# Gated linear attention feeding a GLU: x in place, half-word weights and 29 fillers on one core

## The chip, the cores and the metric

The program runs on one core of one Trainium2 chip. The metric is device time in microseconds (us): the median of three runs of the whole program, and beside it the time of the one execution that the profiler recorded.

The engines by their names in the profile: PE is TensorE's matmul side and PEld its weight loads, DVE is VectorE, ACT is ScalarE, POOL is GpSimd, SP is SyncE. Each engine works through its own queue in order; semaphores tie the queues together.

## The reference, cut to what matters

```python
# q, k, v, alpha: (4, 8, 768, 48) float32: batch, heads, time, channels
for t in range(S):
    state = alpha[:, :, t, :, None] * state + np.einsum('bhd,bhe->bhde', k[:, :, t], v[:, :, t])
    y[:, :, t] = np.einsum('bhd,bhde->bhe', q[:, :, t], state)
# x = y with heads beside each other: (3072, 384)
gate = 1.0 / (1.0 + np.exp(-(x @ w_gate)))      # w_gate, w_val: (384, 1536)
val = x @ w_val
out = (gate * val @ w_out).astype(np.float32)   # w_out: (1536, 384)
```

The three weight matrices arrive as float64.

## The kernel before, in words

**Tiles.** The 3072 tokens are cut into six groups (g) of 512. In a group, the attention comes in four units (p), each of two heads: a unit's heads sit at partitions 0 to 47 and 64 to 111 of a tile of 128. The feed-forward part goes through twelve slices (f) of 128 hidden channels, so there are 72 steps. A step multiplies x of the group (three thirds of 128 channels by 512 tokens) with the slices of w_gate and w_val (line 230), takes the sigmoid on ScalarE (line 625), the product on VectorE (627), splits it into a high and a low part (628, 629), and multiplies these with the slice of w_out into three PSUM banks, `po` (637). Each matrix product is three products of float32r parts: high by high, high by low, low by high. For that x, the weights and the gated values are all kept as a high and a low part.

**A unit** of the first eight (function `unit`, lines 434 to 514) works in chunks of 128 tokens: two scans over the decays on VectorE (381, 385), keys times G (389) and queries times F (447) on VectorE or GpSimd as the tuples `KEYS` and `QUERIES` say, transposes of the keys on TensorE (402) and a ScalarE copy of them (406), matmuls for the state increments (464) and for the scores (459), a mask on VectorE (472), four state updates for each unit on VectorE (487), a multiplication of the states by the decay on GpSimd (495), and the outputs: state part (506) and score part (510) into one PSUM bank, each matmul of float32 operands being two instructions. `finish` (410) copies the output to `yt` on ScalarE (413), moves its rows by DMA into the place in x that they have among 384 channels (420), then casts a full third of x to its high part (427) and subtracts to get the low one (429). The first four units, of group 0, come before all feed-forward work; units 4 to 7 are woven into the steps of group 0, later units (`late`, line 516, in chunks of 64) into those of the groups before theirs.

**Weights** (`weight_piece`, line 328). Each of the twelve slices is loaded in two pieces of 576 columns (slice 0 in three of 384) as pairs of 32-bit words, 25 pieces in all. Two ScalarE passes (342, 343), a sign pass on VectorE or on ScalarE (349, 346, by the tuple `SIGNS`) and a shift-and-or on VectorE (351) turn a float64 into a float32; a ScalarE cast (353) makes the high part and a VectorE subtraction (355) the low one. Raw words go through a ring of four tiles.

**Order.** Nothing is ordered by hand: each piece of work is added to a `Plan` with its engine, an estimated time, a due time, and what it reads and writes. `order` (line 80) simulates the engines and always takes the ready piece with the earliest latest start; `SHIFTS` moves single due times. GpSimd and those VectorE pieces that are marked `port` are kept apart in that simulation. The resulting sequence is what each queue gets.

**Fillers** (`warm`, line 606) are bfloat16 matmuls on the identity matrix whose results nobody reads. There are `WARM` of them, the first eight at once, the others wherever the plan has TensorE idle. They write the PSUM bank that unit 4's transposes use next.

Of the kernel before, what the change touches and what calls it, by code (L numbers as in the profile page):

```python
# [40 lines left out]

WIDTH = EH + 3 * T + 1
# [7 lines left out]
class Plan:  # L50
# [14 lines left out]
    def add(self, engine, time, key, fn, reads=(), writes=(), port=False):  # L65
# [12 lines left out]
        self.parts.append((engine, time, key, fn, deps, port or engine == "gpsimd"))  # L78

    def order(self):  # L80
# [23 lines left out]
        for _ in self.parts:  # L104
            best = None
            for e, ns in waiting.items():
# [5 lines left out]
                if e == "gpsimd" and any(self.parts[m][5] and latest[m] < latest[n] and max(free["vector"], ready_at[m]) < t + self.parts[n][1]  # L112
# [93 lines left out]
def gla_then_glu(ctx: ExitStack, tc: tile.TileContext, q, k, v, alpha, rows, vc, vh, weights_in, out):  # L206
# [9 lines left out]
    with ExitStack() as fast:  # L216
        chunked(fast, tc, rows, vc, vh, weights_in, out, const, ident, flags, weights, within)
# [16 lines left out]
def chunked(ctx, tc, rows, vc, vh, weights_in, out, const, ident, flags, weights, within):  # L234
# [45 lines left out]
    r_v = ring("v", 2, CH, 2, D, early=[borrow("w8", CH, 2, D) for _ in range(2)])  # L280
    raws = [(f"raw{i}", sb.tile([P, WF // 2, 2], U32, name=f"raw{i}")) for i in range(2)]
    for _ in range(2):
        nm, t = borrow("w11", WF // 2, 2)
        raws.append((nm, t.bitcast(U32)))
    r_raw = Ring(raws)
    r_kn = ring("kn", 1, CH, P, early=[borrow("w6", CH, P) for _ in range(2)])
    r_yt = ring("yt", 2, T, early=[borrow("x1", T)])
# [16 lines left out]
    r_bank = Ring([*r_at.tiles, *r_po.tiles, *r_gv.tiles[1:]])  # L304
    ob = [(f"raw{i // 2}", raws[i // 2][1].rearrange("p a b -> p (a b)").bitcast(F32)[:, i % 2 * T:(i % 2 + 1) * T]) for i in range(NM)]
# [15 lines left out]

    plan.add("gpsimd", 1.2, None, later, writes=["later", *(("start", u) for u in range(EARLY))])
# [5 lines left out]
    def weight_piece(f, key):  # L328
        cuts = (0, DM, 2 * DM, WF) if f == 0 else (0, WF // 2, WF)
        over = before(f"w{f}") if f >= 6 else []  # L330
        for i, (lo, hi) in enumerate(zip(cuts, cuts[1:])):
            n = hi - lo
            rn, raw = r_raw.next() if f < NF - 1 else raws[i]
            raw = raw[:, 0:n]
            upper, lower = raw[:, :, 1], raw[:, :, 0]
            halves = raw.bitcast(U16).rearrange("p m (w h) -> p m w h", h=2)
            most, sign = halves[:, :, 0, 1], halves[:, :, 1, 1]
            ru, rl = (rn, "u"), (rn, "l")
            kk = key
            plan.add("sync", (0.475, P * n * 8 / RATE), None, lambda raw=raw, lo=lo, hi=hi: nc.sync.dma_start(  # L340
                out=raw.rearrange("p a b -> p (a b)"), in_=weights_in[f, :, 2 * lo:2 * hi]), writes=[ru, rl])
# [92 lines left out]
    def unit(u, g, p, t):  # L434
# [6 lines left out]
        vn, v = r_v.next()  # L441
        plan.add("sync", (0.475, P * CH * 2 * D * 4 / RATE), after(t["load"], 0.2), lambda: nc.sync.dma_start(
# [434 lines left out]
```

## Time and profile before

| what | value |
|---|---|
| median of 3 runs | 548.3 us (547.92 to 549.14) |
| profiled execution | 548.93 us, span 546.9 us |
| TensorE matmul busy | 537.1 us, 98% |
| TensorE weight load busy | 433.7 us, 79% |
| VectorE busy | 331.5 us, 61% |
| ScalarE busy | 212.5 us, 39% |
| GpSimd busy | 79.6 us, 15% |
| granted TensorE clock, mean | 0.995 |

The span runs from the first instruction to the last; the rest of the execution lies around it. Busy time is the union of the instructions' recorded times on an engine: matmuls overlap in the record, so a busy TensorE can still be waiting on a column count of its own, and a filler counts as busy as much as a product does. Shares over the whole span mix the beginning, where attention and weights keep VectorE and ScalarE full, with the long rest.

### The profile page before, as it was taken

To read this page: it belongs to the slowest core of one execution; us is meant where nothing else is said; L and a number is where in the kernel's file an instruction comes from. 1 tells how busy PE (TensorE), PEld (TensorE's weight loads), DVE (VectorE), ACT (ScalarE), POOL (GpSimd) and SP (SyncE) were. 2 spreads that over 40 slices of the span, in tenths; PEclk is the share of its full clock that TensorE was granted. 3 is DMA by queue.
4 is the path that set the end of the run, shared out by engine and by line. 5 is a ranking of instruction groups with operands and counts; after the bars stand their busy time and mean duration, and the time that the engine had idled before them with its cause. 6 is when DMAs were issued, how large, how long until landed. Compare 5 with 4: busy or idle time off the path is not lost.

```text
span 546.9 us, 10258 instructions
## 1 busy us (share of the span) xinstructions
PE 537.1 (98%) x4150; PEld 433.7 (79%) x4150; DVE 331.5 (61%) x639; ACT 212.5 (39%) x386; POOL 79.6 (15%) x99
## 2 busy tenths in 40 slices
PE   8999999999999999999999999999999999999994
PEld 3767878888888888888888888888888888888883
DVE  7999899995745774546557648557556342222221
ACT  2779899863323233223223323232323222211121
POOL 2412102102202220203202112022021010000000
PEclk9999999999999999999999999999999999999998
DMA  8855787731320321402303403203311000100001
GB/s 306 284 173 182 224 258 209 235 93 63 102 79 25 102 67 37 160 18 84 103 0 103 159 1 103 86 17 102 121 41 50 1 14 16 59 0 0 2 1 64
DMA packets 22120, 51.19 MB, mean 94 GB/s; under 512 B 3504, under 2 KB 8624, under 8 KB 22064
## 3 DMA queue, kind: packets, MB, share of 16 engines
q1 hardware_dynamic: 22064, 50.46, 29.2%
q8 instruction: 34, 0.56, 0.4%
q14 instruction: 22, 0.18, 0.1%
HBM read 41.01 MB, written 4.72 MB: 84 GB/s over the span
## 4 chain that ended last, share of the span: by engine, by line
PE 96%; DMA 1%; SPq 1%; ACT 0%; issue 0%; ACTq 0%
PE gv L230 54%; PE po L637 28%; PE gv L597 3%; PE gv L402 2%; PE at L551 2%; PE gv L608 1%; DMA v<-in_vc_dram 1%; PE at L459 1%; PE at L557 1%; PE gv L506 1%; PE gv L510 1%; SPq L439 1%; PE po L459 0%; PE gv L464 0%; PE at L506 0%; PE po L506 0%
## 5 line engine op out<-in xcount | busy, mean ns | idle before, releaser
L230 PE MATMUL gv<-x,w 128*128 128x512 f32 x1296 | 315.1, 390 | 0.0
L230 PEld LDWEIGHTS gv<-x,w 128*128 128x128 f32 x1296 | 242.9, 188 | 51.1 <-issue 0.4
L627 DVE TENSOR_TENSOR gv<-gv,sg 128x512 f32<-128x512 f32 x72 | 50.5, 701 | 157.4 <-PE gv L230 150.8
L637 PE MATMUL po<-hh,w 128*128 128x512 f32 x432 | 114.1, 395 | 0.0
L628 ACT CAST hh<-gv 128x512 fp32r<-128x512 f32 x72 | 42.9, 595 | 140.3 <-DVE gv L627 133.6
L637 PEld LDWEIGHTS po<-hh,w 128*128 128x128 f32 x432 | 79.4, 188 | 17.1
L625 ACT ACTIVATE sg<-gv 128x512 f32<-128x512 f32 x72 | 43.3, 602 | 115.9 <-PE gv L230 115.9
L585 POOL TENSOR_TENSOR vs<-st,dec 64x384 f32<-64x384 f32 x32 | 35.0, 1095 | 271.7 <-DVE st L580 270.5
L629 DVE TENSOR_TENSOR hl<-gv,hh 128x512 fp32r<-128x512 f32 x72 | 49.7, 690 | 23.4 <-ACT hh L628 21.3
L637 PE MATMUL po<-hl,w 128*128 128x512 f32 x216 | 63.5, 392 | 0.0
L637 PEld LDWEIGHTS po<-hl,w 128*128 128x128 f32 x216 | 40.2, 188 | 8.4
L580 DVE SCALAR_TENSOR_TENSOR st<-st,dec,at 128x48 f32<-128x48 f32 x128 | 33.9, 265 | 4.4 <-PE at L557 0.2
L381 DVE TENSOR_TENSOR_SCAN G<-in,d1g 128x512 f32<-128x512 f32 x22 | 32.2, 1469 | 4.9 <-DMA in<-in_rows_dram 4.2
L567 DVE TENSOR_TENSOR A<-at,mask 64x256 f32<-64x256 f32 x64 | 26.9, 420 | 3.4 <-PE at L557 2.8
L389 POOL TENSOR_TENSOR in<-in,G 128x512 f32<-128x512 f32 x17 | 22.8, 1340 | 35.6 <-DVE G L381 34.8
L385 DVE TENSOR_TENSOR_SCAN F<-in,d1f 128x512 f32<-128x512 f32 x22 | 27.6, 1256 | 0.5
L538 DVE TENSOR_TENSOR A<-A,F 64x512 f32<-64x512 f32 x32 | 24.0, 750 | 0.6
L395 ACT ACTIVATE F<-F 128x512 f32<-128x512 f32 x23 | 14.7, 639 | 17.5 <-DVE A L538 14.8
L597 PE MATMUL gv<-A,vs 128*48 128x64 f32 (+1 forms) x512 | 17.6, 221 | 0.0
L597 PEld LDWEIGHTS gv<-A,vs 128*48 128x48 f32 (+1 forms) x512 | 15.2, 123 | 2.8 <-DVE A L567 2.0
L429 DVE TENSOR_TENSOR x<-x 128x512 fp32r<-128x512 f32 x18 | 12.8, 709 | 6.2 <-ACT x L427 6.2
L608 PE MATMUL gv<-ident 128*128 128x512 bf16 x55 | 15.0, 405 | 0.0
(142 smaller groups left out, 383.7 us busy)
## 6 DMA issues: line engine op xcount, KB each, us to landing
in<-in_rows_dram SPq DMA_DIRECT2D x16, 516.5 KB, 4.2
raw<-in_w_dram SPq DMA_DIRECT2D x12, 576.0 KB, 4.1
first_w<-in_w_dram SPq DMA_DIRECT2D x10, 576.0 KB, 4.7
out_dram<-raw SPq DMA_DIRECT2D x18, 256.0 KB, 2.3
v<-in_vc_dram SPq DMA_DIRECT2D x22, 192.0 KB, 4.8
A<-in_rows_dram SPq DMA_DIRECT2D x32, 128.0 KB, 3.7
x<-yt SPq DMA_DIRECT2D x35, 96.0 KB, 2.6
in<-in_rows_dram SPq DMA_DIRECT2D x4, 772.5 KB, 4.8
```

Source lines behind the costliest of these rows:

```text
L230: nc.tensor.matmul(out=dst, lhsT=lhs(a, i), rhs=rhs(b, i), start=(n == 0 and i == 0), stop=(n == len(todo) - 1 and i == NK - 1))
L381: plan.add("vector", scan(n), t["G"], lambda: nc.vector.tensor_tensor_scan(out=G[:, ::-1], data0=az[:, n:0:-1], data1=d1g[size], initial=0 ...
L385: plan.add("vector", scan(n), after(t["G"], 0.01), lambda: nc.vector.tensor_tensor_scan(out=F, data0=az[:, 0:n], data1=d1f, initial=0.0, o ...
L567: plan.add("vector", 0.43, t["mask"], lambda pa=pa, j=j, i=i: nc.vector.tensor_tensor(out=A[other[j], j].rearrange("p (c i t) -> p i c t", ...
L580: nc.vector.scalar_tensor_tensor(out=st[:, c + 1, :], in0=st[:, c, :], scalar=dec[:, c:c + 1], in1=pas[c % 2][1][:, T // 2 + c // 2 * D:T ...
L585: plan.add("gpsimd", pool_(EH * D), t["sd"], lambda j=j: nc.gpsimd.tensor_tensor(out=vs[own[j], j], in0=st[own[j], 0:EH], in1=dec[own[j]]. ...
L597: nc.tensor.matmul(out=py[R * j:R * j + D, cs], lhsT=vs[r, j, c, :], rhs=A[r, j, cs], start=True, stop=True)
L625: plan.add("scalar", act(T), first(0.3), lambda: nc.scalar.activation(out=sg, in_=got["g"][1][:, 0:T], func=AF.Sigmoid), [got["g"][0]], [sgn])
L627: plan.add("vector", vec(T), first(0.4), lambda: nc.vector.tensor_tensor(out=pv, in0=pv, in1=sg, op=ALU.mult), [sgn], [pvn])
L628: plan.add("scalar", act(T), first(0.45), lambda: nc.scalar.copy(out=hh, in_=pv), [pvn], [hhn])
L629: plan.add("vector", vec(T), first(0.5), lambda: nc.vector.tensor_tensor(out=hl, in0=pv, in1=hh, op=ALU.subtract), [pvn, hhn], [hln])
L637: nc.tensor.matmul(out=pso_now[m][1][:, 0:T], lhsT=weights.part("o", b, f)[:, m * P:(m + 1) * P], rhs=h[a][:, 0:T], start=(f == 0 and i == ...
```

## The change

**x of the first four units in place.** The v of these units is loaded with a gap of 16 zero columns between the heads (`vg`, rows of 112), and the decayed states of the two heads are written into a tile of 96 columns per chunk, zero elsewhere, by two GpSimd multiplications in place of one. The new `in_place` issues the output in three blocks of 32 channels per unit, each into the partitions and the `po` bank where x wants them: 4 x 3 matmuls from the states with 112 rows, then 4 x 2 per head from the scores. The `yt` copy and the DMAs of these units go; high and low part of x are made straight from PSUM. Steps 0 and 1 issue their products one third of x at a time, where they took two thirds and then one. The early units' PSUM ring shrinks from seven banks to four, since `po` holds x.

**Weights from half words.** The float64 array is read as 16-bit words, with a start three half words into the double ahead, so that the 32 bits below a number's top 16 make one aligned word. One cast of the top 16 bits, read as bfloat16, to float16 (ScalarE, or VectorE for the pieces in `CASTS`) gives sign, exponent and first mantissa bits; a shift by 13 and an or on VectorE add the rest. Casts go into `top` tiles, three up to slice 7 and then one.

**Lower parts by DMA.** For the four pieces in `SUMS` the low part is minus the high part, written by ScalarE, to which a DMA issued by GpSimd adds the float32 number.

**Fillers and placement.** 29 fillers in place of 60; keys on VectorE for unit 0 alone, queries for units 0, 4, 5, 6; new due-time shifts; a spacer tile of another size.

```diff
+def ahead(w, f, lo, n):
+    return bass.AP(tensor=w.tensor, offset=w.offset + f * P * WF * 4 + lo * 4 + 3, ap=[[WF * 4, P], [1, 4 * n + 4]])
...
-            plan.add("scalar", 0.02 + n / 960, kk, lambda up=upper.bitcast(F32): nc.scalar.activation(out=up, in_=up, func=AF.Copy, scale=2.0 ** -112), writes=[ru])
-            plan.add("scalar", 0.02 + n / 960, kk, lambda most=most, lower=lower: nc.scalar.activation(
-                out=lower, in_=most, func=AF.Copy, scale=2.0 ** -13, bias=2.0 ** -15 - 0.5), writes=[rl])
-            if (f, i) in SIGNS:
-                plan.add("scalar", 0.08 + n / 500, kk, lambda most=most, up=upper.bitcast(F32): nc.scalar.copy(
-                    out=most.bitcast(F16), in_=up), [ru], [rl])
+            plan.add("sync", (0.475, P * n * 8 / RATE), None, lambda raw=raw, lo=lo, n=n: nc.sync.dma_start(
+                out=raw.bitcast(U16), in_=ahead(weights_in, f, lo, n)), writes=[ru, rl])
+            if (f, i) in CASTS:
+                plan.add("vector", 0.01 + n / 960, kk, lambda high=high, most=most: nc.vector.tensor_copy(out=high, in_=most), [ru], [rt], port=True)
             else:
-                plan.add("vector", 0.01 + n / 960, kk, lambda most=most, sign=sign: nc.vector.tensor_scalar(
-                    out=most, in0=sign, scalar1=0x8000, scalar2=None, op0=ALU.bitwise_and), [ru], [rl], port=True)
-            plan.add("vector", 0.07 + n / 960, kk, lambda upper=upper, lower=lower: nc.vector.scalar_tensor_tensor(
-                out=lower, in0=upper, scalar=3, in1=lower, op0=ALU.logical_shift_left, op1=ALU.bitwise_or), [ru], [rl], port=True)
-            plan.add("scalar", 0.02 + n / 960, kk, lambda lower=lower, lo=lo, hi=hi: nc.scalar.copy(
-                out=weights.tile(f)[:, 0, lo:hi], in_=lower.bitcast(F32)), [rl], [("wh", f, i), *over])
-            plan.add("vector", vec(n), kk, lambda lower=lower, lo=lo, hi=hi: nc.vector.tensor_tensor(
-                out=weights.tile(f)[:, 1, lo:hi], in0=lower.bitcast(F32), in1=weights.tile(f)[:, 0, lo:hi], op=ALU.subtract),
-                [rl, ("wh", f, i)], [("w", f, i)], port=True)
+                plan.add("scalar", 0.08 + n / 500, kk, lambda high=high, most=most: nc.scalar.copy(out=high, in_=most), [ru], [rt])
+            high, low = (weights_part(f, part, lo, hi) for part in range(2))
+            word = raw[:, 0:n]
+            plan.add("vector", 0.07 + n / 960, kk, lambda lower=lower, top=top, word=word: nc.vector.scalar_tensor_tensor(
+                out=word, in0=lower, scalar=13, in1=top, op0=ALU.logical_shift_right, op1=ALU.bitwise_or), [rt, ru], [rl], port=True)
+            word = word.bitcast(F32)
+            plan.add("scalar", act(n), kk, lambda word=word, high=high: nc.scalar.copy(out=high(), in_=word), [rl], [("wh", f, i), *over])
+            if (f, i) in SUMS:
+                plan.add("scalar", act(n), kk, lambda low=low, word=word: nc.scalar.activation(
+                    out=low(), in_=word, func=AF.Copy, scale=-1.0), [rl, ("wh", f, i)], [("w", f, i)])
+                plan.add("gpsimd", (1.0, P * n * 8 / RATE), kk, lambda low=low, word=word: nc.gpsimd.dma_start(
+                    out=low().bitcast(F32), in_=word, accum_op=ALU.add), [rl], [("w", f, i)], port=False)
+            else:
+                plan.add("vector", vec(n), kk, lambda word=word, high=high, low=low: nc.vector.tensor_tensor(
+                    out=low(), in0=word, in1=high(), op=ALU.subtract), [rl, ("wh", f, i)], [("w", f, i)], port=True)
...
-    r_bank = Ring([*r_at.tiles, *r_po.tiles, *r_gv.tiles[1:]])
+    r_bank = Ring([r_gv.tiles[1], *r_at.tiles, r_gv.tiles[2]])
...
+        if not g:
+            in_place(p, t, qT, inn, (vn, vw), (an, A), (sdn, sd), (st, sn), (dec, decn))
+            return
...
+        def from_states():
+            for c in range(CH):
+                for i in range(3):
+                    nc.tensor.matmul(out=at(i, c), lhsT=sd[0:GAP, c, 32 * i:32 * i + 32], rhs=qT[0:GAP, c * C:(c + 1) * C], start=(c == 0), stop=False)
+        def from_scores(j):
+            for c in range(CH):
+                for i, lo in (((0, 0), (1, 32)), ((2, 80), (1, 48)))[j]:
+                    nc.tensor.matmul(out=at(i, c), lhsT=vw[:, c, lo:lo + 32], rhs=A[:, j, c * C:(c + 1) * C], start=False, stop=(c == CH - 1 and (i, j) != (1, 0)))
+        plan.add("tensor", (0.9, 0.5), t["out"], from_states, [(inn, "q"), *((sdn, x) for x in range(4))], banks)
+        for j in range(2):
+            plan.add("tensor", (0.9, 0.5), t["out"], lambda j=j: from_scores(j), [(vn, "v"), (an, j), (an, 2 + j)], banks)
+        if p:
+            kk = p - 1
+            pxn, px = r_po.tiles[kk]
+            plan.add("scalar", act(T), t["y"], lambda: nc.scalar.copy(out=xin(0)[:, kk, 0], in_=px[:, 0:T]), [pxn], [("x0", kk, "h")])
+            plan.add("vector", vec(T), t["y"], lambda: nc.vector.tensor_tensor(
+                out=xin(0)[:, kk, 1], in0=px[:, 0:T], in1=xin(0)[:, kk, 0], op=ALU.subtract), [pxn, ("x0", kk, "h")], [("x0", kk, "l")])
+            xparts.setdefault(0, []).extend([("x0", kk, "h"), ("x0", kk, "l")])
...
-            for tiles in ([range(NK - 1), range(NK - 1, NK)] if s < 2 else [range(NK)]):
+            for tiles in ([range(k, k + 1) for k in range(NK)] if s < 2 else [range(NK)]):
...
-SIGNS = ((0, 0), (1, 1), (2, 0), (2, 1), (3, 1), (4, 1), (5, 1), (6, 0), (6, 1), (7, 1), (8, 1), (9, 0), (11, 0))
-QUERIES = (0, 2, 5, 6)
-KEYS = (0, 1, 3, 4, 5, 7)
-WARM = 60
-APART = 104
+SUMS = ((9, 1), (10, 0), (10, 1), (11, 0))
+CASTS = ((0, 2), (3, 1), (5, 0), (5, 1), (7, 0), (7, 1), (10, 1))
+QUERIES = (0, 4, 5, 6)
+KEYS = (0,)
+WARM = 29
+APART = 24
```

## Rows read from the trace of the kernel before

**Rows 1.** The page, part 1: busy time, share and count by engine.

```profile
PE 537.1 (98%) x4150; PEld 433.7 (79%) x4150; DVE 331.5 (61%) x639; ACT 212.5 (39%) x386; POOL 79.6 (15%) x99
```

**Rows 2.** Windows: stretch, length, busy of PE, PEld, DVE, ACT, POOL, clock, DMA.

```profile
0.00:36.30 36.30, 33.55 (x352) 20.95 (x352) 31.50 (x71) 19.52 (x41) 9.52 (x28) 1.00 0.76 257
36.30:120.00 83.70, 83.70 (x614) 67.64 (x610) 78.71 (x136) 76.41 (x125) 12.49 (x13) 1.00 0.64 201
120.00:540.00 420.00, 419.81 (x3193) 345.07 (x3189) 221.31 (x433) 116.18 (x221) 57.58 (x58) 1.00 0.19 58
```

**Rows 3.** The chain that ended last: start, length, what.

```profile
30.86 3.78 PE gv L608 x17
```

**Rows 4.** Timeline of PE up to the first product: start, length, instruction, idle before.

```profile
2.41 1.49 PE L608 MATMUL po<-ident 128*128 128x512 bf16 x3
3.69 3.88 PE L608 MATMUL gv<-ident 128*128 128x512 bf16 x12
...
28.77 1.08 PE L506 MATMUL po<-first_w,vs 48*48 48x128 f32 x16
29.79 1.08 PE L510 MATMUL po<-first_w,first_w 128*48 128x128 f32 x16
30.80 3.84 PE L608 MATMUL gv<-ident 128*128 128x512 bf16 x17
34.48 0.60 PE L402 MATMUL gv<-ident,in 128*128 128x128 f32 x4
35.81 0.56 PE L464 MATMUL gv<-v,kn 128*48 128x48 f32 x16 [0.73 <-ACT kn L406]
36.30 0.50 PE L230 MATMUL gv<-x,w 128*128 128x512 f32 x1
```

**Rows 5.** Windows of the fillers' line alone: PE, PEld, clock, DMA.

```profile
0.00:14.00 14.00, 9.89 (x32) 3.52 (x32) 1.00 0.85 309
14.00:36.30 22.30, 7.25 (x28) 2.56 (x28) 1.00 0.71 224
```

**Rows 6.** DMA issues: count, KB each, median us to landing.

```profile
raw<-in_w_dram SPq DMA_DIRECT2D x12, 576.0 KB, 4.1
...
x<-yt SPq DMA_DIRECT2D x35, 96.0 KB, 2.6
```

**Rows 7.** Timeline of DVE: last masks of unit 3, last third of x.

```profile
26.70 1.27 DVE L472 TENSOR_TENSOR first_w<-po,mask 128x512 f32<-128x512 f32 x2
...
37.90 0.69 DVE L429 TENSOR_TENSOR x<-x 128x512 fp32r<-128x512 f32 x1
```

**Rows 8.** Groups by line and shape: count, busy us, mean ns, idle before.

```profile
L389 DVE TENSOR_TENSOR in<-in,G 128x512 f32<-128x512 f32 x5 | 3.4, 683 | 0.9 <-DMA in<-in_rows_dram 0.9
L342 ACT ACTIVATE raw<-raw 128x576 f32<-128x576 f32 x12 | 9.3, 776 | 0.0
L346 ACT CAST raw<-raw 128x576 f16<-128x576 f32 x7 | 10.9, 1551 | 0.0
L349 DVE TENSOR_SCALAR raw<-raw 128x576 uint16<-128x576 uint16 x5 | 4.1, 820 | 0.0
L351 DVE SCALAR_TENSOR_TENSOR raw<-raw 128x576 uint32<-128x576 uint32 x12 | 9.5, 793 | 0.5 <-ACT raw L346 0.5
L355 DVE TENSOR_TENSOR w<-raw,w 128x576 fp32r<-128x576 f32 x12 | 9.0, 753 | 0.1
```

**Rows 9.** Timeline about 202 us, and the page's group of that scan.

```profile
202.07 1.28 POOL L389 TENSOR_TENSOR in<-in,G 128x512 f32<-128x512 f32 x1
202.47 1.96 DVE L385 TENSOR_TENSOR_SCAN F<-in,d1f 128x512 f32<-128x512 f32 x1
L385 DVE TENSOR_TENSOR_SCAN F<-in,d1f 128x512 f32<-128x512 f32 x22 | 27.6, 1256 | 0.5
```

**Rows 10.** Timeline: a low weight part on DVE, next products on PE.

```profile
109.48 0.76 DVE L355 TENSOR_TENSOR w<-first_w,w 128x576 fp32r<-128x576 f32 x1
112.96 1.30 PE L230 MATMUL gv<-x,w 128*128 128x512 f32 x5
```

More of the change, by code (lines that the diff above doesn't have):

```diff
@@ L63, in __init__, with add @@
         self.last_write, self.reads_since = {}, {}
-    def add(self, engine, time, key, fn, reads=(), writes=(), port=False):
+    def add(self, engine, time, key, fn, reads=(), writes=(), port=None):
         n = len(self.parts)
@@ L77, in add @@
         deps.discard(n)
-        self.parts.append((engine, time, key, fn, deps, port or engine == "gpsimd"))
+        self.parts.append((engine, time, key, fn, deps, engine == "gpsimd" if port is None else port))
     def order(self):
@@ L216, in gla_then_glu @@
     with ExitStack() as fast:
-        chunked(fast, tc, rows, vc, vh, weights_in, out, const, ident, flags, weights, within)
+        chunked(fast, tc, rows, vc, vh, vg, weights_in.bitcast(U16), out, const, ident, flags, weights, within)
     found = nc.values_load(within[0:1, 0:1], min_val=0, max_val=1)
@@ L231, in products, with chunked @@
                          stop=(n == len(todo) - 1 and i == NK - 1))
-def chunked(ctx, tc, rows, vc, vh, weights_in, out, const, ident, flags, weights, within):
+def chunked(ctx, tc, rows, vc, vh, vg, weights_in, out, const, ident, flags, weights, within):
     nc = tc.nc
@@ L279, in chunked @@
     r_in = ring("in", 2, WIDTH, early=[borrow("w10", WIDTH), borrow("w9", WIDTH)])
[L280 to L285, printed above, removed]
+    r_vg = Ring([borrow(tag, CH, GAP) for tag in ("w8", "w8", "w6", "w6")])
+    r_v = ring("v", 2, CH, 2, D)
+    r_raw3 = Ring([])
+    raws = r_raw3.tiles
+    raws += [(f"raw{i}", sb.tile([P, WF + 2], U32, name=f"raw{i}")) for i in range(2)]
+    for tag in ("w11", "w8"):
+        nm, t = borrow(tag, WF + 2)
+        fourth = nm, t.bitcast(U32)
+        if tag == "w11":
+            raws.append(fourth)
+    r_raw = Ring([*raws, fourth])
+    r_top1 = Ring([("top0", sb.tile([P, WF // 2], U32, name="top0"))])
+    r_top = Ring([*r_top1.tiles, *((nm, t.bitcast(U32)) for nm, t in (borrow("w9", WF // 2), borrow("w10", WF // 2)))])
     r_kn = ring("kn", 1, CH, P, early=[borrow("w6", CH, P) for _ in range(2)])
-    r_yt = ring("yt", 2, T, early=[borrow("x1", T)])
+    r_yt = ring("yt", 1, T)
     r_A = ring("A", 2, 2, T, early=[borrow("x1", 2, T), borrow("w7", 2, T)])
@@ L320, in later @@
             nc.gpsimd.tensor_copy(out=mask[E][lo:lo + E], in_=mask[C][lo:lo + E, lo:lo + E])
+    for nm, t in r_top.tiles:
+        plan.add("gpsimd", 0.7, None, lambda t=t: nc.gpsimd.memset(t.bitcast(F32), 0.0), writes=[(nm, "a")], port=False)
+    for nm, t in r_vs.tiles:
+        plan.add("gpsimd", 0.4, None, lambda t=t: nc.gpsimd.memset(t.rearrange("p j c e -> p (j c e)")[:, 0:CH * 2 * D], 0.0),
+                 writes=[(nm, x) for x in range(4)], port=False)
     plan.add("gpsimd", 1.2, None, later, writes=["later", *(("start", u) for u in range(EARLY))])
@@ L359, in weight, with weights_part @@
+    def weights_part(f, part, lo, hi):
+        return lambda: weights.tile(f)[:, part, lo:hi]
     def weight(nm, f):
@@ L440, in unit @@
                 out=tin[:, lo:hi], in_=rows[g, p, :, lo:hi]), writes=[(inn, m) for m in marks])
-        vn, v = r_v.next()
-        plan.add("sync", (0.475, P * CH * 2 * D * 4 / RATE), after(t["load"], 0.2), lambda: nc.sync.dma_start(
-            out=v.rearrange("p c j e -> p (c j e)"), in_=vc[g, p]), writes=[(vn, "v")])
+        if g:
+            vn, v = r_v.next()
+            plan.add("sync", (0.475, P * CH * 2 * D * 4 / RATE), after(t["load"], 0.2), lambda: nc.sync.dma_start(
+                out=v.rearrange("p c j e -> p (c j e)"), in_=vc[g, p]), writes=[(vn, "v")])
+        else:
+            vn, vw = r_vg.next()
+            plan.add("sync", (0.475, P * CH * GAP * 4 / RATE), None, lambda: nc.sync.dma_start(
+                out=vw.rearrange("p c e -> p (c e)"), in_=vg[p]), writes=[(vn, "v")])
+            v = vw.rearrange("p c (o e) -> p c o e", o=1)
+            v = [vw[:, :, R * j:R * j + D] for j in range(2)]
+        vj = (lambda c, j: v[:, c, j]) if g else (lambda c, j: v[j][:, c])
         kT, qT = tin[:, A_K:A_Q], tin[:, A_Q:WIDTH]
@@ L847, in laid_out @@
     vh = vv.reshape(NG, NP, 2, EH, E, D).transpose(0, 1, 2, 4, 3, 5).reshape(NG, NP, 2, E, EH * D)
+    vg = np.zeros((NP, C, CH, GAP), np.float32)
+    for j in range(2):
+        vg[..., R * j:R * j + D] = vc[0].reshape(NP, C, CH, 2, D)[..., j, :]
     w = np.empty((NF, P, 3, DM), np.float64)
```

46 lines of the change are left out of this document (30 added, 16 removed).

## The prediction

> **What bounds the kernel now.** I read the page's engine line first: TensorE is busy for 98% of the span [rows 1]. Busy says little of what it is busy with, so next the busy times by stage [rows 2]: from 36.3 to 120 us TensorE has no idle time at all, from 120 to 540 us 0.2 us of 420. Only the first 36.3 us, before the first product of the feed-forward part, can hold time that is not work. The chain of waits confirms it: the last stretch in it that is not a product or an attention matmul is a run of 17 fillers at 30.86 us [rows 3], and the timeline of TensorE [rows 4] shows the order at that place: outputs of unit 3 up to 30.80, 17 fillers, unit 4's transposes at 34.48, a wait of 0.73 us for ScalarE's copy, unit 4's adds at 35.81, the first product at 36.30. All 60 fillers lie ahead of 36.3 us, 28 of them behind 14 us [rows 5]. So the kernel's time is (moment from which TensorE is dense) + (dense work, some 504 us, which the change leaves as it is) + tail. The question is how much earlier the dense stretch begins, and whether weights and queries keep up once it does: between 36.3 and 120 us VectorE is 94% busy and ScalarE 91% [rows 2], so the covers there are thin.
>
> **The change part by part.**
>
> Fillers. 31 of 60 go. The 17 of rows 4 take 3.68 us from their first start to the transposes, 0.216 us each: 31 x 0.216 = 6.7 us off TensorE's queue. The early ones are dearer (2.41 to 3.69 us: three in 1.28 us, 0.427 each, the lower clock level), but 29 still cover that part. Fillers are no work, but they stood where TensorE waited; they give time back only if what it waited for comes earlier. That is the next part.
>
> x in place. Before, unit 3's last output at 30.80 us is followed by a ScalarE copy, DMAs into x (2.6 us each from issue to landing [rows 6]), a ScalarE cast and a VectorE subtraction, which ran at 37.90 us [rows 7]: 7 us from output to the last third of x. After, the outputs land in PSUM at the row where x wants them: cast and subtraction remain, and as products now go by thirds of x, the first two thirds (units 0 to 2) start the step. Without the DMA the chain is 0.6 + 0.7 us and hand-overs, about 1.5 us: the wait that the 17 fillers hid goes. This costs TensorE: per unit 16 + 16 output matmuls become 24 + 32 (four chunks, three blocks from the states, two blocks per head from the scores, two instructions each). The rows show 16 in 1.02 and 16 in 1.01 us [rows 4], two at a time side by side in the two column halves. The 32 score matmuls take 2.03 us at that rate, what both kinds took before. The 24 state matmuls go to three column groups: if three run side by side 24 x 0.063 x 2/3 = 1.0 us, if two, 1.5 us; one change of array shape per unit goes, so I take 0.9 us, for four units +3.6 us. Bounds: 0 where they fall into waiting time; above, all 56 one after the other at a transpose's 0.15 us (0.60 us for four [rows 4]), 8.4 us in place of 2.03, +25 us for four units.
>
> Step 0 behind unit 4. The 0.73 us wait for the copy before unit 4's adds stands between fillers and products; with x ready, products can lie there: -0.7 us (bounds 0 and -0.7).
>
> Keys and queries. Keys of units 1, 3, 4, 5, 7 move from VectorE (0.68 us) [rows 8] to GpSimd (1.28 us [rows 9]), one query each way. Ahead of the first product that takes 3 x 0.68 = 2.0 us from VectorE, whose last mask of unit 3 began at 26.70 and ended by 28.0 [rows 7]. It must now prepare there what it did later: two subtractions for x and the second weight piece, about 2.5 us at 0.7 a piece. So masks end at about 28.5, the last scores' matmuls, cast and subtraction follow by 31, and the products of the first two thirds (12, at little more than a filler's 0.216) can begin 2.7 us before that, near 28.3. TensorE's own sum gives 36.30 - 6.7 + 3.6 - 0.7 = 32.5 with unit 4's two small groups ahead, about 31.5 without. The later of the two holds: TensorE's queue.
>
> Weights. Per piece of 576, two ScalarE passes (0.776, the second alike), a sign pass (VectorE 0.82 or ScalarE 1.55), an or (0.79), a cast and a subtraction (0.75) [rows 8] become one 16-bit cast (ScalarE in 18 of 25 pieces, VectorE in 7), the or, the cast and the subtraction; in four pieces the last is a scaled ScalarE copy and an adding DMA. ScalarE: -50 x 0.77 + 5 x 1.55 + 4 x 0.75 = -28 us; VectorE: -5 x 0.82 - 4 x 0.75 = -7.1 us; with keys 4, 5, 7 and the query of unit 4, -8.4 us. All of it lies beside TensorE's dense stretch, so in itself it is worth nothing; it pays for the earlier start, for which VectorE has 3.8 us less time. If the cover were gone, TensorE would wait for weights.
>
> The adding DMA has no like in the trace. Its piece is 288 KB within SBUF; the nearest rows are the 96 KB move into x, 2.6 us, and the 576 KB weight load, 4.1 us [rows 6]; I take 3.5 us, in place of a 0.75 us subtraction. The slack: a subtraction ended at 110.24 us and the next step's products began at 112.96 us [rows 10], 2.7 us. The ScalarE relief comes ahead of it, so I cost it at nothing. Memsets on GpSimd, the larger v tiles, fewer raw and PSUM buffers: beside other work, nothing, up to 0.5 us each way.
>
> A row speaks against the keys on GpSimd: at 202.07 a key multiplication there met an F scan on VectorE, and the scan took 1.96 us [rows 9] where the mean is 1.256: 0.70 us longer. Five more keys, each meeting one, take 3.5 us of the 8.4 us relief. The Trainium skill (SBUF — State Buffer, section "SBUF: two separate sides") says that VectorE and GpSimd take a shared port pair as an exclusive lock, and the loser blocks fully; the trace agrees with 0.70 us of blocking. By that rule, if the whole 1.28 us were blocked five times, the relief would shrink by 6.4 us. The same section warns that descriptors of DMAs that GpSimd issues wait while VectorE holds that pair; no run here shows it yet.
>
> **Sum**, on the profiled execution's 548.93 us (span 546.9 and 2.0 around it): -6.7 + 3.6 - 0.7 = -3.8, so 545.1; the median of the runs is 0.6 lower, 548.3: 544.5 us.
>
> **Rivals.**
> A. VectorE, not TensorE's queue, sets the start, as the idle time that fillers leave is larger than I think: dense from about 29 us rather than 31.5 or 32.5, some 3 us more, 541.5. For it: the 28 late fillers [rows 5]. Against: TensorE's own outputs grow.
> B. The clock. With fewer fillers TensorE idles before step 0 and the first products run at the lower level, as the early fillers did: ten at 0.427 instead of 0.216, +2.1 us, 546.6. Against: from 14 us on four units keep it busy.
> C. VectorE is too late in steps 0 to 3 because GpSimd holds it up: 3.5 us of lost VectorE time becomes TensorE waits of 1.5 to 3.5 us: 546 to 548. For it: 94% busy.
> D. Slower: the four lower parts land late. They feed steps 9, 10 and 11; each landing L us after the subtraction would have ended holds TensorE for L - 2.7 us, and its order is fixed. Over three steps the gain is gone at L = 4.0; at L = 5, 3 x 2.3 = 6.9, so 551.4. Against: ScalarE's 28 us of relief let the copies run earlier.
> E. The 32-column blocks don't run side by side: four units at up to 8.4 us; less 2 us of waiting, +19 to 23 us against my 3.6: about 562. The rows' side-by-side halves speak against it.
>
> **How the numbers follow.** Forecast 0.53 (own range 542.5 to 546), A 0.20, B 0.11, C 0.08, D 0.06, E 0.02. The range 540.5 to 547.2 leaves out D, E, part of C and the far end of A. Less than 0.2% (1.1 us) cannot be told from no change here. Faster: forecast, A, most of B and half of C, 0.86; same: the rest of B and C, 0.07; slower: D and E, little of C, 0.07.
>
> **What would show it.** First product at 30 to 33 us in TensorE's timeline; 29 fillers, none of them in a run of 17 next to it; no DMA from yt in front of it and a third of x about 1.5 us after its last output; four units' outputs at about 2.9 us; no TensorE wait in steps 0 to 11 and VectorE under 90% there; full clock at the first product; the adding DMAs landed before steps 9 to 11 begin. A first product at 36 us, or TensorE idle over 2 us after it, would make the prediction wrong.

## The result: slower, 552.14 us against 549.01 us

Measured side by side, the changed kernel takes 552.14 us (median of 10 executions, 550.43 to 553.25), the kernel before 549.01 us: ratio 1.0057, 95% interval 1.0044 to 1.0071. The forecast was 544.5 us, the range ended at 547.2 us; the sign was wrong. Three of the ten executions had a mean granted clock of 0.998 or 0.999 and took 550.43 to 551.66 us (median 550.64), seven had 0.991 to 0.994 and took 551.96 to 553.25 us: some 1.5 us of the 3.1 is the clock, the rest is there at full clock. The profiled execution, one of the three, took 550.64 us with a span of 548.9 us, 2.0 us more than the one before. The page of it, part 1, beside [rows 1]:

```profile
PE 535.9 (98%) x4215; PEld 433.6 (79%) x4215; DVE 326.5 (59%) x625; ACT 179.9 (33%) x341; POOL 96.7 (18%) x117
```

ScalarE lost 33 us of work (28 forecast), VectorE 5 (8.4), GpSimd gained 17. By stage (windows as in [rows 2]):

```profile
0.00:36.30 36.30, 33.04 (x415) 22.93 (x415) 29.74 (x64) 14.07 (x31) 21.47 (x41) 1.00 0.71 254
36.30:120.00 83.70, 81.08 (x546) 64.12 (x547) 72.99 (x129) 48.36 (x89) 16.57 (x18) 1.00 0.69 209
120.00:540.00 420.00, 420.00 (x3252) 345.44 (x3250) 223.10 (x434) 116.26 (x220) 58.66 (x58) 1.00 0.19 58
```

TensorE, without a gap from 36.3 to 120 us before, now has 2.6 us of idle time there. The timeline of TensorE in the changed kernel (start, length, instruction, idle before and its releaser) shows where; it answers to [rows 4]:

```profile
25.48 1.94 PE L576 MATMUL po<-first_x,first_w 128*32 128x128 f32 x32
27.36 0.96 PE L236 MATMUL gv<-x,w 128*128 128x512 f32 x3
...
29.39 1.34 PE L571 MATMUL po<-first_w,vs 112*32 112x128 f32 x24
30.66 0.96 PE L236 MATMUL gv<-x,w 128*128 128x512 f32 x3
31.55 1.94 PE L576 MATMUL po<-first_w,first_w 128*32 128x128 f32 x32
33.42 1.68 PE L236 MATMUL gv<-x,w 128*128 128x512 f32 x6
34.95 0.60 PE L427 MATMUL gv<-ident,in 128*128 128x128 f32 x4
36.27 0.56 PE L497 MATMUL gv<-v,kn 128*48 128x48 f32 x16 [0.73 <-ACT kn L431]
36.77 5.81 PE L236 MATMUL gv<-x,w 128*128 128x512 f32 x24
42.42 0.60 PE L427 MATMUL gv<-ident,in 128*128 128x128 f32 x4
43.75 1.16 PE L492 MATMUL at<-in 48*128 48x128 f32 x16 [0.74 <-DVE in L480]
45.47 0.56 PE L497 MATMUL gv<-v,kn 128*48 128x48 f32 x16 [0.55 <-ACT kn L431]
46.89 0.49 PE L710 MATMUL po<-hh,w 128*128 128x512 f32 x1 [0.86 <-ACT w L371]
47.59 1.42 PE L710 MATMUL po<-hh,w 128*128 128x512 f32 x5 [0.20 <-DVE w L378]
```

The first product starts at 27.36 us, 8.9 us earlier than before, and 12 products are done when the kernel before begins its first. The thirteenth starts at 36.77 us, against 39.20 us before (from the starts of the single products): TensorE is 2.4 us ahead, behind a wait for unit 4's keys. Then it waits for unit 4's query, for unit 5's keys, and for a weight piece. For the first product of step 12 it is 2.0 us behind (128.19 us against 126.18 us), and from there the two kernels run alike.

To see where those 2.0 us are made, I took for each TensorE instruction the time to the next one's start and summed it by kind up to step 12. Fillers, with what TensorE waits behind them: 16.6 us before, 8.2 after, -8.4. Outputs of units: 15.9 to 21.2, +5.35. All else, which does the same work in both and so holds the waits: +5.1. Together +2.0.

### The profile page after: what moved, and what is told of

It reads as the page before. It is cut to its first block, busy times and chain, and to the rows that moved or that the text cites. A ratio compares the mean times of both kernels' runs of the same rounds, so it can differ in the third digit from the quotient of the medians.

```text
span 548.9 us, 10350 instructions
## 1 busy us (share of the span) xinstructions
PE 535.9 (98%) x4215; PEld 433.6 (79%) x4215; DVE 326.5 (59%) x625; ACT 179.9 (33%) x341; POOL 96.7 (18%) x117
## 4 chain that ended last, share of the span: by engine, by line
PE 96%; DVE 1%; POOL 1%; issue 0%; ACT 0%; POOLq 0%; ACTq 0%
PE gv L236 54%; PE po L710 27%; PE gv L670 3%; PE gv L427 2%; PE at L624 2%; PE at L630 1%; PE gv L681 1%; PE po L576 1%; PE at L492 1%; PE gv L542 1%; PE gv L546 1%; PE po L571 1%; PE gv L497 0%; POOL first_w L480 0%; PE po L681 0%
## 5 line engine op out<-in xcount | busy, mean ns | idle before, releaser
L658 POOL TENSOR_TENSOR vs<-st,dec 64x384 f32<-64x384 f32 x32 | 36.4, 1139 | 262.4 <-DVE st L653 246.7
L406 DVE TENSOR_TENSOR_SCAN G<-in,d1g 128x512 f32<-128x512 f32 x22 | 34.0, 1548 | 1.9 <-DMA in<-in_rows_dram 1.9
L414 POOL TENSOR_TENSOR in<-in,G 128x512 f32<-128x512 f32 x21 | 29.2, 1391 | 29.4 <-DVE G L406 26.3
L431 ACT COPY kn<-gv 128x512 f32<-128x512 f32 x21 | 12.3, 586 | 9.6 <-PE gv L427 7.5
L438 ACT COPY yt<-gv 128x512 f32<-128x512 f32 x20 | 11.7, 586 | 10.0 <-PE gv L670 7.4
```

The costliest lines, as they stand in the source:

```text
L406: plan.add("vector", scan(n), t["G"], lambda: nc.vector.tensor_tensor_scan(out=G[:, ::-1], data0=az[:, n:0:-1], data1=d1g[size], initial=0 ...
L414: plan.add(e, vec(n) if u in KEYS else pool_(n), t["kt"], lambda: getattr(nc, e).tensor_tensor(out=kT, in0=kT, in1=G, op=ALU.mult), [gn, ( ...
L658: plan.add("gpsimd", pool_(EH * D), t["sd"], lambda j=j: nc.gpsimd.tensor_tensor(out=vs[own[j], j], in0=st[own[j], 0:EH], in1=dec[own[j]]. ...
```

## The experiments

Ratios are to the kernel before, measured beside it on the same chip (medians of 548.4 to 549.0 us). In the expectations O is the theory that the order of the instructions, fixed by durations and due times, doesn't fit the changed kernel; C is the clock, D the adding DMAs, P the hold that VectorE and GpSimd have on each other.

**e1_again.** The changed kernel, no edit.

> The changed kernel as it is, for a second trace beside the first (span 548.9 us, 1.7 us over the profiled run before, while the median of ten runs was 3.1 over). Theory O (the written order: the third weight piece of slice 0 is prepared too late, TensorE waits in steps 0 and 1): ratio 1.005 to 1.007, the same waits between 43 and 50 us, 2.5 to 3.5 us over the usual. Theory C (clock: with fewer fillers TensorE falls to its lower level somewhere in the first 50 us in many executions): the trace shows a second low stretch, some 3 to 4 us, in executions that take 551 us and more. Theory D (the adding DMAs): TensorE waits at steps 9 to 11; the first trace shows none.

551.91 us, ratio 1.0065 [1.0045, 1.0086]: the loss is repeated. Two of its four executions had a mean granted clock of 0.998 and spans of 549.2 and 549.4 us, two had 0.991 and 0.993 and spans of 551.6 and 550.9 us.

**e2_noshift.** No due time is shifted.

```diff
-SHIFTS = (
...
+SHIFTS = ()
```

> All due-time shifts taken out, everything else as changed, so that the plan orders by its own due times. O: the waits of 43 to 50 us go (3 us) and some of those between 18 and 37 us; ratio 0.993 to 1.000. C: the time stays above that of before by about the clock's part, ratio 1.002 to 1.005, with runs some us apart. D: no change, 1.005, since the four DMAs are still there. P (GpSimd's keys and queries hold VectorE up): no change, 1.004 to 1.006.

550.26 us, 1.0028 [1.0017, 1.0039]. Better than the changed kernel, but above the range of theory O: the shifts as a set do not fit, and no shifts do not either.

**e3_one_shift.** One entry is taken out, the one that delays VectorE's 16-bit cast of the third weight piece.

```diff
-SHIFTS = (... (153, -6), (164, 13), (192, -2), ...)
+SHIFTS = (... (153, -6), (192, -2), ...)
```

> One entry of 49 is taken out: the one that moves the due time of VectorE's cast of the third piece of slice 0 by 13 steps' time. O: this cast runs some 8 us earlier than at 44.9 us, the wait at the first product with w_out (46.9 us, 0.9 us, and three after it) goes: 2 to 3 us off, ratio 1.000 to 1.002. C, D, P: no change, 1.004 to 1.007.

549.03 us, 1.0002 [0.9992, 1.0012]: of one due time some 3 us come back, in theory O's range. The plan orders with this entry, so other parts change places too. The two profiled executions, both at full clock, differ by 1.5 us in span (548.9 and 547.4 us); the rest is the clock, which no execution of e3 lost (0.996 to 0.998 in all ten). The four rows of the changed kernel behind it (VectorE, ScalarE):

```profile
44.88 0.38 DVE L363 CAST first_w<-first_w 128x384 f16<-128x384 bf16 x1
45.75 0.55 DVE L368 SCALAR_TENSOR_TENSOR first_w<-first_w,first_w 128x384 uint32<-128x384 uint32 x1
46.99 0.55 DVE L378 TENSOR_TENSOR w<-first_w,w 128x384 fp32r<-128x384 f32 x1
```

```profile
46.33 0.51 ACT L371 CAST w<-first_w 128x384 fp32r<-128x384 f32 x1 [0.92 <-DVE first_w L368]
```

The piece had been loaded by a DMA issued before 13 us; its cast stood in VectorE's queue until 44.88 us, behind unit 5's scan of G (35.57 us) and a wait of 0.98 us, and the products that need it began at 46.89 us. Nothing made it late but its place in the queue.

**e4_no_sums.** No adding DMA; VectorE subtracts for all pieces.

```diff
-SUMS = ((9, 1), (10, 0), (10, 1), (11, 0))
+SUMS = ()
```

> No piece by an adding DMA: VectorE subtracts in all 25. The shifts stay; the due times of what leads to those four pieces become later, and by that the plan puts the cast of the third piece of slice 0 some 8 us earlier. D in its plain form (they land late): nothing to gain, as no wait stands there. O: the DMAs cost through the order alone; ratio 0.996 to 1.001. C: 1.003 or above. P: 1.004 to 1.006.

549.98 us, 1.0023 [1.0013, 1.0033], between the ranges of O and C, but the order changed with it; e12 repeats it with an order of its own.

**e5_fillers_in_waits.** Three fillers ahead of each of four waits, all else in the same order.

```diff
         for n in self.order():
+            if n in (296, 295, 351, 315):
+                for _ in range(3):
+                    self.filler()
             self.parts[n][3]()
...
```

> The changed kernel with its order unchanged; three fillers (0.65 us) are put ahead of the parts in front of which TensorE waited longest after 36 us: at 36.3 (0.98 us), 43.8 (0.95), 45.5 (0.80) and 46.9 (0.85 us). Theory C (some executions of the changed kernel run at a mean granted clock of 0.991 to 0.994 and are 1.5 us longer because TensorE stands idle there): no execution under 0.996 any more, the median falls by about 1.5 us, to 550.4, ratio 1.003. Theory O (only the time that TensorE waits for the preparations matters): the fillers lie inside the waits, nothing is gained, 551.9, ratio 1.0055 to 1.0065, and the executions still fall in two kinds. If they stood on the path: 4 x 0.65 = 2.6 us more, 554.5.

551.48 us, 1.0044 [1.0028, 1.0060]. No execution under a clock of 0.996 (five of five), as theory C has it, but the median fell by 0.4 us where it expected 1.5: so part of the fillers' 2.6 us was paid, by this reading.

**e8_second_look.** The changed kernel once more, to see the clock by stage.

> The changed kernel once more, for the granted clock by stage. Theory C: if this execution falls in the longer kind (mean clock 0.991 to 0.994, span 550.2 to 551.6), the trace shows a stretch at half clock between 36 and 60 us, where TensorE waited six times; if it falls in the shorter kind (0.998, span 548.6 to 549.9), none is there.

553.17 us, span 551.4 us, mean clock 0.991. TensorE's timeline, then windows (as above; the third number from the end is the granted clock):

```profile
44.24 1.16 PE L492 MATMUL at<-in 48*128 48x128 f32 x16 [0.77 <-DVE in L480]
45.96 0.57 PE L497 MATMUL gv<-v,kn 128*48 128x48 f32 x16 [0.55 <-ACT kn L431]
47.38 3.20 PE L710 MATMUL po<-hh,w 128*128 128x512 f32 x6 [0.86 <-ACT w L371]
```

```profile
44.00:46.00 2.00, 1.20 (x18) 1.01 (x19) 2.00 (x5) 1.91 (x5) 0.00 (x0) 1.00 0.05 17
46.00:48.00 2.00, 1.14 (x17) 0.69 (x17) 2.00 (x6) 1.18 (x2) 0.00 (x0) 0.70 0.64 175
48.00:50.00 2.00, 2.00 (x6) 1.53 (x6) 2.00 (x7) 0.57 (x2) 0.21 (x1) 0.50 0.64 187
50.00:52.00 2.00, 2.00 (x6) 1.61 (x5) 1.93 (x6) 0.45 (x2) 0.79 (x2) 0.50 0.60 228
52.00:54.00 2.00, 2.00 (x7) 1.54 (x6) 1.99 (x3) 1.25 (x2) 0.00 (x0) 0.59 0.92 265
```

TensorE waits 0.77, 0.55 and 0.86 us, and the clock is at half (1.2 GHz) from about 46.8 us, within the third of these waits, to 53.6 us. The span is 2.5 us longer than that of the first trace, which has nearly the same waits (0.74, 0.55 and 0.86 us) and a clock of 1.00 there. Of the 15 executions of the changed kernel 10 had a mean clock of 0.991 to 0.994; the kernel before never had less than 0.995 where its clock is on record.

**e7_before_29.** The kernel before with 29 fillers, the entries of `SHIFTS` renumbered to the same parts.

```diff
-WARM = 60
+WARM = 29
```

> The kernel before, its due times renumbered, with 29 fillers in place of 60, the only edit. Theory W (the 31 fillers lay inside waits of TensorE for the units, and cost nothing): the time stays, 548.0 to 549.5, ratio 0.998 to 1.002, and waits of about 6.7 us appear ahead of 36.3 us in place of the fillers. Theory F, that of the prediction (fillers are a term of the sum): -6.7 us, 542.1, ratio 0.988. Theory C (the idle time lets the clock fall): 550 to 552, with executions at a mean clock under 0.996.

553.36 us, 1.0081 [1.0065, 1.0096]: slower by over 4 us, at mean clocks of 0.988 to 0.990. TensorE's timeline:

```profile
37.10 0.88 PE L464 MATMUL gv<-v,kn 128*48 128x48 f32 x16 [5.71 <-ACT kn L406]
```

As the order is planned from the durations, it had changed too, so:

**e13_before_29_same_order.** The 31 fillers are not issued, every other instruction keeps its place.

```diff
-        plan.add("tensor", (0.2135, 1.0), i - 2000.0 if i < 8 else 2000.0, lambda: nc.tensor.matmul(
+        plan.add("tensor", (0.2135, 1.0), i - 2000.0 if i < 8 else 2000.0, lambda: i < 29 and nc.tensor.matmul(
```

> The kernel before with the last 31 of its 60 fillers not issued and every other instruction on every engine in the order that it had. Theory F, that of the prediction (fillers are a term of the sum): -6.7 us, 542, ratio 0.988. Theory W (they covered a wait for ScalarE's copies of x and of unit 4's keys): the first product stays within 0.5 us of 36.30 us and the time within 1 us of the kernel before if the clock holds. Theory C (the idle time lets the clock fall, as in the run with 29 fillers, where ten microseconds ran at half clock): the first product at 36 to 37 us, then 5 to 10 us at half clock, 551 to 554, ratio 1.004 to 1.010.

549.78 us, 1.0020 [1.0007, 1.0033]. TensorE, then windows:

```profile
31.02 0.66 PE L402 MATMUL gv<-ident,in 128*128 128x128 f32 x4 [1.52 <-DVE in L389]
34.58 0.89 PE L464 MATMUL gv<-v,kn 128*48 128x48 f32 x16 [2.90 <-ACT kn L406]
35.40 9.89 PE L230 MATMUL gv<-x,w 128*128 128x512 f32 x35
```

```profile
32.00:34.00 2.00, 0.00 (x0) 0.00 (x0) 2.00 (x4) 1.91 (x5) 0.00 (x0) 0.53 0.21 52
34.00:36.00 2.00, 1.42 (x18) 1.23 (x19) 2.00 (x7) 2.00 (x4) 0.00 (x0) 0.50 0.54 134
36.00:38.00 2.00, 2.00 (x6) 1.62 (x5) 2.00 (x5) 2.00 (x5) 0.00 (x0) 0.50 1.02 408
38.00:40.00 2.00, 2.00 (x8) 1.55 (x8) 2.00 (x6) 1.09 (x2) 1.35 (x2) 0.76 0.43 119
```

Where the 17 fillers of [rows 4] had stood, TensorE waits 1.52 us for unit 4's key (VectorE, which has no idle time here) and 2.90 us for its copy. The first product comes at 35.40 us instead of 36.30 us: the 31 fillers cost 0.9 us, not 6.7. And the clock is at half from about 32.1 to 39.0 us; TensorE works in 4.4 us of these (from 34.58 us on), an estimated loss of 2.2 us. In the trace the lead is 1.2 us at unit 4's adds (34.58 against 35.81 us) and 0.9 at the first product, and from the thirteenth product on TensorE is 0.7 us behind (39.90 against 39.20 us). The time is 1.1 us (by the ratio) to 1.4 us (by the medians) above the kernel before. Theory F is refuted; of W the covered waits hold, of C the clock, though with less loss than expected.

**e6_half_scores.** On e3: half of the score matmuls of the in-place outputs are left out.

```diff
         def from_scores(j):
-            for c in range(CH):
+            for c in (0, CH - 1):
```

> As the kernel with one due time given back (549.03 us, ratio 1.0002), but of the 32 score matmuls per unit in the in-place outputs the 16 of the two middle blocks of rows are left out (the outputs of units 0 to 3 lack that part). Theory I (in the first 36 us TensorE's own queue sets the start of the dense stretch, so the in-place outputs, 1.3 us a unit dearer than before, stand in the sum): 4 x 16 x 0.063 = 4.0 us less, 545.0, ratio 0.993. Theory P (VectorE and GpSimd, which hold each other up, set it, so that TensorE would only wait longer for the next part): under 1.5 us less, 547.5 or more, ratio 0.9975 or more.

546.61 us, 0.9962 [0.9949, 0.9976]: 2.2 us less than e3 by the ratios (2.4 by the medians) for 4.0 us less of TensorE's work, between the theories. All else keeps its order. In-place outputs stand on the path for a little over half; the rest turns into waiting.

**e10_less_vector.** On e3: for slices 0 and 1 no subtraction on VectorE.

```diff
-            if (f, i) in SUMS:
+            if f <= 1:
+                plan.add("scalar", act(n), kk, lambda low=low, word=word: nc.scalar.activation(
+                    out=low(), in_=word, func=AF.Copy, scale=-1.0), [rl, ("wh", f, i)], [("w", f, i)])
+            elif (f, i) in SUMS:
```

> As the kernel with one due time given back (549.03 us), but for the weights of slices 0 and 1 VectorE's subtraction (three of 0.55 us, two of 0.75 us) is left out: ScalarE writes a scaled copy there and nothing is added to it (the lower parts of these weights are wrong). Theory V (VectorE's preparation of units and weights sets when TensorE can go on in the first 50 us): 3.15 us less work there, 1.5 to 3.2 us less time, 545.9 to 547.5. Theory I (TensorE's own queue sets it): within 0.5 us of 549.0.

546.35 us, 0.9966 [0.9953, 0.9979]: 2.0 us less than e3 by the ratios (2.7 by the medians) for 3.15 us less on VectorE. That is in theory V's range, and I is refuted as expected. Windows from 36.3 to 60 us, first e3, then e10: TensorE's 1.8 us of idle time are gone.

```profile
36.30:60.00 23.70, 21.89 (x156) 16.82 (x156) 21.96 (x45) 15.04 (x27) 3.37 (x5) 1.00 0.61 206
```

```profile
36.30:60.00 23.70, 23.70 (x164) 18.89 (x163) 22.82 (x44) 15.58 (x29) 4.08 (x6) 1.00 0.81 270
```

The plan gave e10 another order too: unit 4's transposes stand at 31.11 us, ahead of unit 3's outputs, in e3 at 35.72 us, behind them. So it isn't shown how much of the 2 us is VectorE's missing work and how much the order.

**e9_keys_back.** On e3: keys and queries on the engines that the kernel before has for them.

```diff
-QUERIES = (0, 4, 5, 6)
-KEYS = (0,)
+QUERIES = (0, 2, 5, 6)
+KEYS = (0, 1, 3, 4, 5, 7)
```

> As the kernel with one due time given back (549.03 us), but keys and queries go to the engines on which the kernel before has them (keys of units 0, 1, 3, 4, 5 and 7 and queries of 0, 2, 5 and 6 on VectorE). Theory P (GpSimd's keys and queries hold VectorE up: its operations before 126 us take 5.1 us more than the shortest of their form there, 1.0 in the kernel before): VectorE gets 4 us back and pays 5 x 0.68 = 3.4 us for the keys, 0.5 us less in all or none, 548.5 to 549.1. Theory V (the number of operations on VectorE ahead of the first products is what counts, 3 x 0.68 = 2.0 us more): 550.5 to 551.1, ratio 1.003 to 1.004.

556.24 us, 1.0129 [1.0108, 1.0149]; both theories missed it by 5 us or more. TensorE's timeline:

```profile
31.90 0.41 PE L571 MATMUL po<-first_w,vs 112*32 112x128 f32 x2 [2.18 <-POOL vs L558]
...
38.34 1.66 PE L236 MATMUL gv<-x,w 128*128 128x512 f32 x6
...
46.60 1.96 PE L236 MATMUL gv<-x,w 128*128 128x512 f32 x6 [1.88 <-DVE st L520]
```

The due times had been made for other engines; the first product is at 38.34 us. The clock falls as well: windows of 2 us from 34 and from 48 us have 0.53 and 0.50, and all four executions a mean clock of 0.989 to 0.993. The run says nothing on the keys, and e14 was made for that.

**e11_new_order.** The changed kernel, only its due times shifted anew; no instruction differs.

```diff
-SHIFTS = (
...
+SHIFTS = (
...
```

> The changed kernel with no instruction added or taken away: only the due times of 252 parts are shifted anew, so that the engines' orders fit the changed durations. Theory O (the changed kernel lost its gain because parts of the weights and of units 4 and 5 stand in the wrong order): below the 549.03 us that one due time gave back, 544 to 548, ratio 0.990 to 0.998, with fewer than three TensorE waits over 0.6 us after 36 us. If TensorE and VectorE both have their full work in the first 50 us and no order is better: 548.5 to 549.5.

547.37 us, ratio 0.9977 [0.9969, 0.9986] (12 executions, one of 1366.89 us, which nothing here explains, the others between 546.95 and 548.12). That is some 4.5 us below the changed kernel, and 1.3 us below the kernel before; no mean clock is under 0.997. After 36 us one wait over 0.4 us is left:

```profile
45.76 0.56 PE L497 MATMUL gv<-v,kn 128*48 128x48 f32 x16 [0.45 <-ACT kn L431]
```

**e12_new_order_no_adds.** As e11 without adding DMAs (`SUMS = ()`), with an order of its own.

> As the kernel with all due times shifted anew, but without the adding DMAs (VectorE subtracts for all pieces, 4 x 0.75 us more there, 4 x 0.67 less on ScalarE), with due times (263) of its own. Theory D (the adding DMAs and their 0.86 to 1.0 us of GpSimd each help or harm): 1 us or more away from the kernel with all due times shifted anew; if VectorE has that time to spare at steps 5 to 8: within 0.5 us of it.

547.77 us, 0.9992 [0.9983, 1.0000]; 0.4 us (medians) to 0.8 us (ratios) above e11: with an order of its own for each, the adding DMAs show no harm and help a little at most.

**e14_keys_back_new_order.** As e9 (keys and queries back), with due times of its own.

> The changed kernel with keys and queries on the engines that the kernel before has for them, and with due times (277) of its own. To be compared with the changed kernel with all due times shifted anew (547.37 us, ratio 0.9977). Theory V (VectorE's work ahead of 50 us sets the time: three keys ahead of the first product and two behind it at 0.68 us): 1.5 to 3 us more, 549 to 550.5, ratio 1.001 to 1.004. Theory P (GpSimd's keys hold VectorE up by as much as they take from it): within 0.7 us of 547.4, ratio 0.9965 to 0.999.

547.53 us, 0.9984 [0.9975, 0.9993]; the same as e11 within the intervals, in theory P's range; V is refuted. With an order of its own for each, where keys and queries run makes no difference that shows. Against e9 an order that fits made 8 us, part of them the clock's (0.997 and 0.998 here).

## Why the prediction was wrong

The step that failed is the rule that holds the sum together: that what goes from TensorE's queue before the dense stretch comes off the time, while the dense stretch stays "as it is" and weights, keys and queries beside it cost nothing. The start came forward, by 2.4 us at the thirteenth product where the sum has 3.8. But by step 12 TensorE is 2.0 us behind: the 4.4 us between were lost where the sum has no term, at waits for unit 4's query, unit 5's keys and weight pieces (2.6 us of it idle time in the record), and the clock took more in most executions. The same instructions in another order (e11) are 4.5 us faster. The sign that the prediction named for itself, TensorE idle over 2 us behind the first product, came: 2.6 us.

**Fillers, -6.7.** The prediction itself said that fillers give time back only if what TensorE waited for comes earlier, and then entered all 31 in full. e13 shows what they are worth alone: 0.9 us of start, and a clock fall in their place. They covered waits for VectorE's and ScalarE's preparation of unit 4; a wait for x, which the prediction saw there, does not show in e13. "98% busy" and "no idle time" were read with fillers counted as work; a row of 17 fillers in the chain of waits is a wait by another name. In the changed kernel products of step 0 took their place: by the account above fillers give 8.4 us and outputs take 5.35, together -3.05, where the sum has -3.1. Both terms were some 1.7 us too small, and that they cancel is luck. No run has x in place with 60 fillers, so what each is worth beside the other stays open.

**x in place, +3.6.** The way from output to third of x is short as worked out: unit 3's scores end at 33.42 us, and VectorE's subtraction for the last third starts at 34.30 us and takes 0.68. Products on earlier thirds run from 27.36 us, sooner than the 30 to 33 us forecast. Three column groups do run side by side; unit 0's state matmuls, with the next start at 12.41 us, take the 1.0 us forecast:

```profile
11.40 1.08 PE L571 MATMUL po<-in,vs 112*32 112x128 f32 x24
```

The 32 score matmuls take 1.87 us (31.55 to 33.42), 2.03 forecast. Even so the four units' outputs take 1.3 us more each, not 0.9: the state matmuls of units 2 and 3 last 1.46 and 1.27 us, and 0.77 us is a wait for a query on GpSimd behind unit 1's scores. Of TensorE's work there a little over half counts (e6).

**Step 0 behind unit 4, -0.7.** The wait stayed, with the same 0.73 us, at 36.27 us, and more came behind it. "No TensorE wait in steps 0 to 11" is what the prediction named as its test, and it fell there.

**Weights, nothing.** ScalarE's relief came, 33 us for 28; VectorE's was 5 us for 8.4. Mean times by shape (count, busy us, mean ns, idle before), in place of those of [rows 8]:

```profile
L371 ACT CAST w<-raw 128x576 fp32r<-128x576 f32 x14 | 9.4, 674 | 9.8 <-DVE raw L368 9.7
L378 DVE TENSOR_TENSOR w<-raw,w 128x576 fp32r<-128x576 f32 x11 | 8.3, 752 | 0.8 <-ACT w L371 0.7
L368 DVE SCALAR_TENSOR_TENSOR raw<-raw,top 128x576 uint32<-128x576 uint32 x9 | 7.0, 782 | 2.4 <-ACT top L365 2.4
L365 ACT CAST top<-raw 128x576 f16<-128x576 bf16 x6 | 5.1, 853 | 2.5 <-DMA raw<-in_w_dram 1.5 <-DVE first_w L368 1.0
```

ScalarE's 33 us bought nothing by themselves, because TensorE had not waited from 36.3 to 120 us before; ScalarE's rows now wait 9.7 us for VectorE's or. Behind the start VectorE is what is full. Windows, first the kernel before, then the changed one:

```profile
36.30:60.00 23.70, 23.70 (x166) 18.94 (x163) 21.25 (x39) 21.80 (x36) 4.67 (x6) 1.00 0.65 217
```

```profile
36.30:60.00 23.70, 21.09 (x151) 16.35 (x152) 22.15 (x45) 13.00 (x25) 2.96 (x5) 1.00 0.60 204
```

ScalarE falls from 21.80 to 13.00 us of 23.70, VectorE rises from 21.25 to 22.15: the scans, masks and states of the units and two operations per weight piece are left on it, and the earlier products want the pieces earlier. That its work, and not only the order of it, holds TensorE is what e10 speaks for (2.0 us for 3.15 us of its work), but the order moved with it. The prediction had the figure (94% busy) and the sentence "VectorE has 3.8 us less time", but priced it in rival C alone. No run has the old weight path in the changed kernel.

**The order.** No rival was an order that doesn't fit. One due time was worth some 3 us (e3), all of them 4.5 us (e11), the clock that no longer fell included. With an order fitted to it the changed kernel is 0.23%, 1.3 us, below the kernel before, a third of what was forecast. The kernel before was given no new order of this kind, so how much of the 1.3 us is the change and how much the fitting is not shown.

**The clock.** Rival B had the mechanism, but not the place: not ahead of step 0, but at 46.8 us in the one trace that caught it, and 10 of 15 executions have a mean clock as low. Between the two kinds of execution lie some 1.8 us in the mean of their spans (548.6 to 549.9 us, 550.2 to 551.6 us); without that fall the changed kernel is still 2 us slower. That the first fillers ran at the lower level, as rival B has it, rests on their 0.427 us alone; the granted clock of that stretch in [rows 5] is 1.00.

**Keys on GpSimd (rival C).** The hold is there: GpSimd's key, then VectorE's product of four columns beside it:

```profile
32.00 1.70 POOL L414 TENSOR_TENSOR in<-in,G 128x512 f32<-128x512 f32 x1 [1.95 <-DVE G L406]
```

```profile
32.48 1.23 DVE L412 TENSOR_TENSOR dec<-in,G 128x4 f32<-128x4 f32 x1
```

The same product took 0.16 us at 40.44 us. The Trainium skill (SBUF — State Buffer, section "SBUF: two separate sides") has the loser block fully, and this row agrees: the product lasts until GpSimd's key ends. Before 126 us four VectorE operations are over 0.2 us longer than the shortest of their form, by 4.4 us together; in the kernel before three are, by 1.0. The difference, 3.4 us, is what the prediction took (3.5). But moving the keys back does not end the hold: the same count gives 6.3 us in e11 and 6.9 us in e14, with this scan as its largest:

```profile
103.55 2.88 DVE L410 TENSOR_TENSOR_SCAN F<-in,d1f 128x512 f32<-128x512 f32 x1
```

Both take 547.4 to 547.5 us. No run is without the hold, so what it costs stays open.

**Adding DMAs (rival D).** They land 3.6 to 4.4 us after their issue (3.5 taken), and no product waited for them at steps 9 to 11; the issue takes GpSimd 0.85 to 1.0 us. Count, KB each, median us to landing, beside [rows 6]:

```profile
w<-raw POOLq DMA_DIRECT2D x3, 288.0 KB, 4.4
w<-first_w POOLq DMA_DIRECT2D x1, 288.0 KB, 3.6
```

Left open: how much of e11's remaining distance to the forecast is TensorE's own dearer outputs and how much VectorE. On e3, e6 and e10 each took away some of one and gained 2.2 and 2.0 us; both together, and either in the order of e11, were not tried.

## What to carry to other kernels

Count fillers as waiting time: before crediting their removal, ask which engine's result the instruction behind them needs, and take them out with all else in place to see. Where an order is fixed by hand or by planned durations, a change of durations is measured only after the order has been fitted again; here that was worth more than the change. The kernel that it is compared with needs the same fitting, which this one did not get. A wait of TensorE costs twice when the clock falls behind it, so a short run of fillers in a wait can be worth its place: with them (e5) none of five executions had a mean clock under 0.996.

## What the runs showed of the hardware

The clock was at half for about 6.8 us in e13 from 32.1 us, behind an idle time of 1.52 us, 0.66 us of work and the first 0.5 us of a wait of 2.90 us; and for as long in e8 from 46.8 us, behind waits of 0.77 and 0.55 us and within one of 0.86 us. The same program with nearly the same waits kept a clock of 1.00 in its first trace, and a mean clock of 0.998 or more in 5 of 15 executions. A VectorE operation on 4 columns can last 1.23 us beside a GpSimd operation on 512, where it took 0.16 us alone. Matmuls into three groups of 32 columns overlap: 24 in 1.01 us (11.40 to 12.41 us), 0.042 us each, where 16 in two groups took 1.01 us.
